# Retention followed by a multiplicative feed-forward layer: 2048-byte query rows, one marker copy per step, and a reordered start

## The chip, the cores and the metric

One core of one Trainium2 chip runs the whole program. The metric is the device time of one execution in microseconds; lower is better. The time before is 187.18 us, the median of three runs (186.01 to 188.56).

## What is computed

For 4 batches and 8 heads with 768 tokens of 64 numbers, a state of 64 x 64 numbers per head decays by a factor and takes in one key and one value per token; each query reads it. The heads of a token then stand side by side as a row of 512 numbers, which goes through four matrices.

```python
gamma = 1.0 - 2.0 ** (-5.0 - np.arange(H))          # H = 8, D = 64, S = 768
for t in range(S):
    state = gamma * state + outer(k[:, :, t], v[:, :, t])
    y[:, :, t] = 1/sqrt(D) * (q[:, :, t] @ state)
x = y.transpose(0, 2, 1, 3).reshape(B * S, H * D)   # 3072 x 512
out = ((x @ w1) * (x @ w2)) @ w3 @ w_out            # 512 -> 1024 -> 1024 -> 512
```

All inputs and the output are float32; the kernel computes its products in fp16 with float32 sums.

## The kernel before

The 3072 tokens are worked in twelve steps of 256 tokens, three for each batch. The order of all work is written out by hand, engine by engine, in the program text: every call of a helper issues its instructions at that place of its engine's queue.

**The start.** w3 and w_out are multiplied into one 1024 x 512 matrix, kept as eight tiles `W3O`. For this the rows of w3 are loaded (`load_rows`, L95), cast to fp16 (`cast_w3`, L228), turned by TensorE (`turn_w3`, L233), copied out of PSUM (`turned_w3`, L240), multiplied with the cast rows of w_out (`cast_wo`, `w3_mm`, L244) and copied out (`w3_out`, L257). Meanwhile GpSimd makes index tables and masks (`numbers`, `keeps`, `late_numbers`, `step_decays`), and ScalarE makes decay tables with the exponential (`tables` for the first two steps, `late_tables`, L215, for the later ones). `warm` (L610) issues products of zeros; eight of them stand at the very start.

**The loads.** SP's queue issues every transfer. `load` (L77) fetches 256 tokens of q, k or v as a tile of 128 partitions x 1024 float32 numbers from a ring of 18 such stage buffers. For the queries, and for all three inputs in steps 0 and 1 (`n < EO`), partition p holds the tokens 2p and 2p + 1 of each of the eight heads, in runs of 512 bytes (L84). For the keys and values of later steps partition i holds token i of each half of the 256, in runs of 256 bytes, with two transfers per tile (L89). Loads, turns and stores of several steps share the one queue in the order written: in the later steps it reads, per step, the turn of k for the next step, v of the step after that, the turn of q, k and q of a step further on, and the store of an earlier result.

**One step.** GpSimd casts q and k to fp16 (`cast`, L266) and scales and casts v (`cast_v`, L278). From step 4 on a DMA transposes the cast tiles into `qT` and `kT` (`dma_turn`, L297, L300); before that TensorE does it (`turn`, `turned`). `kv` (L364) makes the sums of outer products, `state` (L397) carries the state on, `scores` (L324) makes the products of keys and queries, `mask` (L347) cuts the future off. `inter` (L428) multiplies queries with the states; it has two halves, `part` 0 and 1, which write the two halves of the partitions of the same PSUM banks. Between them `fence` (L457) lets ScalarE copy one column of each of the two banks to a scratch tile (L463), and the second half waits for these marker copies. `av` (L465) adds the products of the masked scores with the values, and `x_out` (L486) scales the result into `XT`, the 512 x 256 input of the feed-forward layer. The products of 64 x 64 numbers run four at a time in the quarters of TensorE's array. `qchunk` (L320) cuts the queries of 64 tokens out of `qT`, as two runs of 32 numbers.

**The feed-forward layer.** `blk` with `evac` makes two of the eight row blocks of x @ w1 or x @ w2 (`two_blocks`, L511, L517): 64 products of 128 x 256 per step. VectorE multiplies the two into `HT`. `o_unit` (L567, L572) makes 128 rows of the output with eight products of 128 x 512, `o_copy` scales them, `o_store_all` (L599, L601) stores a step's 256 rows. From step 2 on TensorE's queue goes, per step: the first half of `inter` for step n, the first half of `kv` and the `scores` for n + 1, the second half of `inter`, `av`, the two `o_unit` of step n - 1, and then the `blk` of step n. Steps 0 and 1 use the same products spread out by rows of w1 and w2 as those land (`rows`, L541, L552).

Of the kernel before, what the change touches and what calls it, by code (L numbers as in the profile page):

```python
# [20 lines left out]
def kernel(  # L21
# [15 lines left out]
    EO = 2  # L37
# [39 lines left out]
    def load(nm, n, via=None):  # L77
        via = via or nc.sync
        b, c = divmod(n, PER)
        t = new_stage()  # L80
        src = source[nm][b, :, c * T : (c + 1) * T, :]
        if nm == "q" or n < EO:

            via.dma_start(  # L84
                t[:, :].rearrange("p (h x) -> p h x", x=2 * D), src.rearrange("h (p t) d -> p h (t d)", t=2)
            )
        else:
            for s in range(2):
                via.dma_start(  # L89
                    t[:, s * 512 : (s + 1) * 512].rearrange("p (h d) -> p h d", d=D),  # L90
                    src[:, s * 128 : (s + 1) * 128, :].rearrange("h i d -> i h d"),
                )
        tok_in[nm, n] = t
# [43 lines left out]
    def numbers():  # L137

        nc.gpsimd.iota(key_i[:, :, :], pattern=[[1, 2], [0, H]], base=1 - 128, channel_multiplier=2)
        nc.gpsimd.iota(  # L140
            col_i[:, :, :].rearrange("p g (t j) -> p g t j", t=2), pattern=[[128, 2], [1, 2], [2, 64]],
            base=1 - 128, channel_multiplier=0,
        )
        for h in range(H):
            p = h // 2
            c = place(p, h % 2) * 64
            nc.gpsimd.memset(LGH[:, h : h + 1], -math.log(gam[h]))
            nc.gpsimd.memset(LGP[c : c + 64, p : p + 1], math.log(gam[h]))

    def keeps():  # L150
        nc.gpsimd.memset(keep[:, :, :], 1.0)
        for g in range(2):
            rows = slice(g * 64, g * 64 + 64)
            for t in range(2):
                nc.gpsimd.affine_select(
                    out=keep[rows, t, :], in_=keep[rows, t, :], compare_op=GE, fill=0.0,
                    base=-t, pattern=[[1, 2], [2, 64]], channel_multiplier=-2,
                )

    def late_numbers():  # L160

        nc.gpsimd.iota(tok_i[:, :, :], pattern=[[128, 2], [0, H]], base=1 - 128, channel_multiplier=1)
        for g in range(2):
            nc.gpsimd.iota(
                pos_i[:, g, :, :].rearrange("p s (t i) -> p s t i", t=2), pattern=[[128, 2], [1, 2], [2, 32]],
                base=1 - 128 + 64 * g, channel_multiplier=0,
            )
        nc.gpsimd.memset(keep64[:, :], 1.0)
        for g in range(2):
            rows = slice(g * 64, g * 64 + 64)  # L170
            nc.gpsimd.affine_select(
                out=keep64[rows, :], in_=keep64[rows, :], compare_op=GE, fill=0.0,
                base=0, pattern=[[1, 2], [2, 32]], channel_multiplier=-1,
            )

    VS = const.tile([128, 2, H], FP, name="VS")
# [48 lines left out]
    def cast_wo(i, eng):  # L225
        copy(eng, WO[i][:, :, :].rearrange("p a n -> p (a n)"), wo_st[i][:, :])
# [39 lines left out]
    def cast(nm, n, eng):  # L266
        dst = {"q": q16, "k": k16}[nm]
        dst[n] = t = att.tile([128, 2, 512], HP, tag=nm + "16", name=nm + "16", bufs=3)
        src = tok_in.pop((nm, n))
        if nm == "q" or n < EO:  # L270
            copy(
                eng, t[:, :, :].rearrange("p t (h d) -> p h t d", d=D),
                src[:, :].rearrange("p (h t d) -> p h t d", t=2, d=D),
            )
        else:
            copy(eng, t[:, :, :].rearrange("p s c -> p (s c)"), src[:, :])
# [40 lines left out]
    def half(x):  # L317
        return slice(x * 64, x * 64 + 64)

    def qchunk(n, r, a, s, g):  # L320
        c = 2 * s + g
        return qT[n][half(r), :, a, c * 32 : (c + 1) * 32]

    def scores(n, tags, hp=None):  # L324
        if n < EO:
            ps = [bank(t, [128, 2, 2, 128]) for t in tags]
            for i in range(2):
                for t in range(2):
                    for r, g in QUARTERS:
                        a = hp * 2 + i  # L330
                        nc.tensor.matmul(
                            ps[r][half(g), i, t, :], lhsT=kT[n][half(r), t, a, half(g)],
                            rhs=qT[n][half(r), :, a, half(g)], start=True, stop=True,
                        )
        else:
            ps = [bank(t, [128, NP, 2, 64]) for t in tags]
            for a in range(NP):
                for s in range(2):
                    for r, g in QUARTERS:
                        nc.tensor.matmul(  # L340
                            ps[r][half(g), a, s, :], lhsT=kT[n][half(r), s, a, half(g)],
                            rhs=qchunk(n, r, a, s, g), start=True, stop=True,
                        )
        for r in range(2):
            am[n, hp, r] = ps[r]
# [82 lines left out]
    def inter(n, part, tags=None):  # L428
        assert state_n.get(n, 0) >= len(chunks(n)) - 1 and inter_n.get(n, 0) == part
        if part == 0:  # L430
            for g in range(2):
                X[n, g] = bank(tags[g], [128, NP, 128])
            X[n] = set()
        else:
            assert n in fenced
        inter_n[n] = part + 1
        begun = X[n]
        for i in range(NP // 2):
            for s in range(1 if n < EO else 2):
                for a in (2 * i, 2 * i + 1):  # L440
                    for g in range(2):
                        c = g if n < EO else (s, g)
                        if (n, c) not in TS:
                            continue
                        r = g ^ 1 ^ part
                        o = place(a, r)
                        if n < EO:
                            dst, rhs = X[n, g][half(o), a, :], qT[n][half(r), :, a, half(c)]
                        else:
                            dst, rhs = X[n, g][half(o), a, s * 64 : (s + 1) * 64], qchunk(n, r, a, s, g)  # L450
                        nc.tensor.matmul(  # L451
                            dst, lhsT=TS[n, c][half(r), a, :], rhs=rhs, start=((g, o) not in begun), stop=False,
                            skip_group_check=True,
                        )
                        begun.add((g, o))

    def fence(n):  # L457
        assert inter_n[n] == 1
        fenced.add(n)
        for g in range(2):  # L460
            if (g, g) in X[n]:
                t = att.tile([128, 1], FP, tag=f"fence{g}", name="fence")
                nc.scalar.copy(t[half(g), :], X[n, g][half(g), NP - 1, 64:65])  # L463

    def av(n):  # L465
        assert inter_n[n] == 2
# [19 lines left out]
    def x_out(n, g):  # L486
# [3 lines left out]
            XT[n] = att.tile([128, NP, T], HP, tag="xt", name="xt", bufs=3)  # L490
        x = X.pop((n, g))
        if n < EO:
            order = "p a (t i) -> p a t i"
            nc.vector.tensor_tensor(
                XT[n][:, :, g * 128 : (g + 1) * 128].rearrange("p a (i t) -> p a t i", t=2),
                x[:, :, :].rearrange(order, t=2), YS[:, g, :, :].rearrange(order, t=2), MULT,
            )
        else:
            nc.vector.tensor_tensor(  # L499
                XT[n][:, :, :].rearrange("p a (s x) -> p (a s) x", s=2)[:, :, g * 64 : (g + 1) * 64].rearrange(  # L500
                    "p k (i t) -> p k t i", t=2
                ),
                x[:, :, :].rearrange("p a (s t i) -> p (a s) t i", s=2, t=2),
                YN[:, g, :, :, :].rearrange("p a s (t i) -> p (a s) t i", t=2), MULT,
            )


# [165 lines left out]
    warm(8)  # L673
    identity()
    numbers()
    keeps()
    arguments()
    tables()
    cast_w3(4, "v")
    step_decays()  # L680
    turn_w3(4, "S0")
    late_numbers()
    cast_wo(0, "v")
    turned_w3(4, "s")
    late_arguments()
    w3_mm(4, 0, "S0", first=True)
    cast_w3(1, "v")
    late_tables()
    turn_w3(1, "S1")
    cast_w3(2, "g")  # L690
    turned_w3(1, "v")
    turn_w3(2, "X0")
    cast_wo(1, "g")
    w3_mm(1, 0, "S1", first=True)
    turned_w3(2, "s")
    w3_mm(1, 1)
    cast_w3(5, "v")
    w3_mm(4, 1)
    w3_mm(2, 1, "X0", first=True)
    w3_mm(2, 0)  # L700
    cast_wo(2, "g")
    turn_w3(5, "X1")
    turned_w3(5, "s")
    w3_mm(4, 2)
# [51 lines left out]
    w3_mm(6, 3, last=True)  # L756
    state(0, 1)
    w3_out(7, "s")
    inter(0, 0, ("S0", "X1"))
    fence(0)  # L760
    turn("q", 1, "S1")
# [114 lines left out]
    cast("q", 3, "g")  # L876
    turned("k", 3, "s")
    o_copy(1, 0)
    o_unit(1, 1, ("F2",))
    inter(2, 1)  # L880
    av(2)
    x_out(2, 0)
    x_out(2, 1)
    turn("q", 3, "S1")
    turned("q", 3, "v")
    cast_v(3, "g")
# [448 lines left out]
```

## Time and profile before

| what | value |
|---|---|
| median of three runs | 187.18 us (186.01 to 188.56) |
| the profiled execution, its own time | 186.13 us |
| its span, first to last instruction | 184.4 us |
| granted TensorE clock, mean | 0.991 |
| TensorE (PE) busy | 173.6 us, 94% |
| VectorE (DVE) busy | 97.7 us, 53% |
| ScalarE (ACT) busy | 67.5 us, 37% |
| GpSimd (POOL) busy | 66.6 us, 36% |
| DMA packets | 81,498, 40.23 MB, mean 218 GB/s |
| of these under 512 B, under 2 KB | 59,328 and 75,968 |
| q loads | 12 transfers of 512 KB, median 6.7 us from issue to landing |
| k and v loads | 40 of 256 KB (5.5 and 5.8 us), 4 of 512 KB (10.3 and 9.5 us) |
| turns of k and q by DMA | 8 and 8, 7.0 and 4.9 us |

The durations come from one profiled execution, whose span leaves out 1.7 us of its time. Engines work at the same time, so their busy times do not add up. A wait counts only where the engine that waits is one that others wait for.

### The profile page before, as it was taken

The page shows a single profiled execution, that of the slowest core. Times are in us where ns is not written, and L with a number is a line of the kernel's source. Part 1 is how long each engine was busy: PE and PEld are TensorE (multiplying, and loading weights), DVE is VectorE, ACT ScalarE, POOL GpSimd, SP SyncE. Part 2 cuts the span into 40 slices and gives each one's busy share as a digit, 9 for nine tenths or more (in the row PEclk, how much of TensorE's full clock was granted, in tenths as well). Part 3 has the DMA queues.
Part 4 walks back from the last instruction along what each step waited for, and adds up shares of the span by engine and source line. Part 5 has one row for each costly group of instructions (what it writes and reads, how often), then busy time and mean ns, then how long its engine had stood idle before and what let it go on. Part 6 is the DMA issues. An engine that isn't in the chain of part 4 may idle for free.

```text
span 184.4 us, 6033 instructions
## 1 busy us (share of the span) xinstructions
PE 173.6 (94%) x2616; PEld 124.1 (67%) x2616; DVE 97.7 (53%) x169; ACT 67.5 (37%) x126; POOL 66.6 (36%) x93
## 2 busy tenths in 40 slices
PE   7489999898999799999999999999999999999993
PEld 2255555577955587685885868858778587686872
DVE  2433689842745485738447465472673844644220
ACT  4634415664253421331333233323133142332332
POOL 7851248653546136726244235440354010000000
PEclk9969999999999999999999999999999999999999
DMA  5999999999999899999999999999999960150303
GB/s 203 368 420 360 320 302 326 400 349 236 181 256 247 183 167 231 193 183 245 167 236 231 169 285 200 229 244 183 271 222 178 243 228 4 36 195 4 116 0 114
DMA packets 81498, 40.23 MB, mean 218 GB/s; under 512 B 59328, under 2 KB 75968, under 8 KB 81472
## 3 DMA queue, kind: packets, MB, share of 16 engines
q1 hardware_dynamic: 81472, 39.85, 95.8%
q8 instruction: 20, 0.33, 0.8%
q14 instruction: 6, 0.05, 0.1%
HBM read 29.36 MB, written 6.29 MB: 193 GB/s over the span
## 4 chain that ended last, share of the span: by engine, by line
PE 73%; DMA 8%; SPq 7%; DVE 4%; POOL 3%; ACT 2%; issue 2%; DVEq 0%; ACTq 0%; POOLq 0%
PE psF L517 36%; PE psF L572 20%; DMA st<-in_k_dram 5%; SPq L97 5%; DMA st<-in_moe_w_dram 3%; PE psF L552 3%; PE psX L451 2%; PE psX L552 2%; SPq L84 2%; PE psX L572 2%; PE psS L340 2%; PE psX L478 1%; ACT w L61 1%; DVE t L64 1%; POOL v L64 1%
## 5 line engine op out<-in xcount | busy, mean ns | idle before, releaser
L517 PE MATMUL psF<-xt,w 128*128 128x256 f16 x640 | 72.0, 273 | 1.2 <-DVE xt L499 1.0
L517 PEld LDWEIGHTS <-w 128*128 128x128 f16 x640 | 62.5, 98 | 10.8 <-issue 1.6
L64 DVE TENSOR_TENSOR ht<-pa,psF 128x512 f16<-128x512 f32 x43 | 29.5, 686 | 45.4 <-PE psF L517 43.9
L61 ACT COPY pa<-psF 128x512 f32<-128x512 f32 x43 | 25.1, 585 | 45.4 <-PE psF L517 39.1
L572 PE MATMUL psF<-w3o,ht 128*128 128x512 f16 (+2 forms) x184 | 38.5, 361 | 0.1
L572 PEld LDWEIGHTS <-ht 128*128 128x128 f16 x208 | 19.1, 98 | 19.1 <-DVE xt L499 0.4
L64 POOL TENSOR_TENSOR v<-st,VN 128x1024 f16<-128x1024 f32 x10 | 19.0, 1901 | 24.5 <-DMA st<-in_v_dram 15.8
L590 ACT ACTIVATE osb<-psF 128x512 f32<-128x512 f32 (+2 forms) x22 | 12.3, 558 | 35.1 <-PE psF L572 35.1
L499 DVE TENSOR_TENSOR xt<-psX,YN 128x512 f16<-128x512 f32 x19 | 12.8, 720 | 7.2 <-PE psX L478 7.2
L64 POOL TENSOR_TENSOR t<-s,GS 128x256 f16<-128x256 f32 x8 | 5.8, 728 | 25.2 <-DVE s L64 25.1
L552 PEld LDWEIGHTS <-w 128*128 128x128 f16 x128 | 11.9, 98 | 4.3 <-POOL w L61 1.3
L61 POOL CAST k<-st 128x1024 f16<-128x1024 f32 x11 | 11.4, 1036 | 8.3 <-DMA st<-in_k_dram 8.3
L61 POOL CAST q<-st 128x1024 f16<-128x1024 f32 x11 | 11.4, 1039 | 7.4 <-DMA st<-in_q_dram 4.9
L357 DVE TENSOR_TENSOR am<-psS,keep 128x512 f16<-128x512 f32 x19 | 12.2, 679 | 1.3 <-PE psF L340 1.3
L252 PEld LDWEIGHTS <-w3t 128*128 128x128 f16 x64 | 5.7, 101 | 7.3 <-ACT w3t L61 1.6
L552 PE MATMUL psF<-xt,w 128*128 128x256 f16 x56 | 9.7, 273 | 0.0
L451 PEld LDWEIGHTS <-t 64*64 64x64 f16 x320 | 5.7, 106 | 4.6 <-issue 2.9
L451 PE MATMUL psX<-qT,t 64*64 64x64 f16 (+1 forms) x296 | 8.3, 199 | 0.4 <-DVE t L64 0.2
L237 PEld LDWEIGHTS <-w3h 128*128 128x128 f16 x64 | 4.6, 113 | 4.9 <-DVE w3h L61 3.3
L552 PE MATMUL psX<-xt,w 128*128 128x256 f16 x32 | 6.1, 274 | 1.2 <-POOL w L61 0.6
L61 DVE CAST w3h<-st 128x1024 f16<-128x1024 f32 x5 | 3.5, 701 | 5.8 <-DMA st<-in_moe_w_dram 5.8
L64 DVE TENSOR_TENSOR t<-psK,t 128x256 f16<-128x256 f32 x15 | 6.2, 415 | 0.4
(121 smaller groups left out, 183.1 us busy)
## 6 DMA issues: line engine op xcount, KB each, us to landing
st<-in_moe_w_dram SPq DMA_DIRECT2D x16, 512.0 KB, 8.6
st<-in_q_dram SPq DMA_DIRECT2D x12, 512.0 KB, 6.7
st<-in_k_dram SPq DMA_DIRECT2D x20, 256.0 KB, 5.5
st<-in_v_dram SPq DMA_DIRECT2D x20, 256.0 KB, 5.8
out_dram<-osb SPq DMA_DIRECT2D x9, 512.0 KB, 5.5
st<-in_moe_w_out_dram SPq DMA_DIRECT2D x4, 512.0 KB, 7.8
st<-in_k_dram SPq DMA_DIRECT2D x2, 512.0 KB, 10.3
st<-in_v_dram SPq DMA_DIRECT2D x2, 512.0 KB, 9.5
```

Source lines behind the costliest of these rows:

```text
L61: {"v": nc.vector.tensor_copy, "g": nc.gpsimd.tensor_copy, "s": nc.scalar.copy}[eng](dst, src)
L64: (nc.vector if eng == "v" else nc.gpsimd).tensor_tensor(dst, a, b, op)
L97: nc.sync.dma_start(t[:, :], src[i * 128 : (i + 1) * 128, :])
L237: nc.tensor.transpose(ps[:, g * 128 : (g + 1) * 128], src[:, c0 : c0 + 255 : 2], ident16[:, :])
L252: nc.tensor.matmul(acc[f][:, :], lhsT=w3t[f][:, g * 128 : (g + 1) * 128], rhs=WO[i][:, r, :], start=(first and r == 0), stop=(last and r = ...
L357: nc.vector.tensor_tensor(t[:, :, :, :].rearrange("p a s i -> p (a s) i"), ps[:, :, :, :].rearrange("p a s i -> p (a s) i"), keep64[:, :]. ...
L451: nc.tensor.matmul(dst, lhsT=TS[n, c][half(r), a, :], rhs=rhs, start=((g, o) not in begun), stop=False, skip_group_check=True,)
L499: nc.vector.tensor_tensor(XT[n][:, :, :].rearrange("p a (s x) -> p (a s) x", s=2)[:, :, g * 64 : (g + 1) * 64].rearrange("p k (i t) -> p k ...
L517: nc.tensor.matmul(ps[:, i, :], lhsT=W[d][:, f * 128 : (f + 1) * 128], rhs=XT[n][:, d, :], start=(i == 0 and d == 0), stop=(i == 1 and d = ...
L552: nc.tensor.matmul(rows_ps[w, n, uh][j // 2][:, j % 2, :], lhsT=W[d][:, f * 128 : (f + 1) * 128], rhs=XT[n][:, d, :], start=(first and j % ...
L572: nc.tensor.matmul(ps[:, :], lhsT=HT[n][:, f, tb * 128 : (tb + 1) * 128], rhs=W3O[f][:, c0:c1], start=(f == 0), stop=(f == 7),)
L590: nc.scalar.activation(o_tile(n, tb)[:, c0:c1], o_ps.pop((n, tb, c0, c1))[:, :], AF.Copy, scale=final_scale)
```

## The change

- **Query loads.** A query tile is loaded by two transfers instead of one, one for the even heads and one for the odd heads. A partition now holds eight tokens of one head, 2048 bytes in one run: 4 heads x 32 groups of tokens make the 128 partitions. The cast puts even and odd heads of the same token side by side, so that the turned tile holds the tokens in eight groups (token modulo 8), and for each group the four head pairs with 32 tokens.
- **What follows from that order.** `queries` takes the place of `qchunk`: eight runs of 16 numbers in steps 0 and 1, eight runs of 8 numbers later. The column tables, the masks and the reading order of `x_out` follow the new order of tokens; `x_out` writes every eighth number in a row instead of every second.
- **Marker copies.** `fence` copies one column of one bank instead of two, and the second half of `inter` takes the two banks in the opposite order.
- **The start.** Some casts and copies change engines; `keeps`, `step_decays` and `late_numbers` stand later in GpSimd's queue, `late_arguments` and `late_tables` behind `w3_out(7)`; ten more products of zeros stand in TensorE's queue between the first turns of w3.
- **One moved block.** `o_unit(1, 1)` stands behind `x_out(2)` instead of before the second half of `inter(2)`.

```diff
         src = source[nm][b, :, c * T : (c + 1) * T, :]
-        if nm == "q" or n < EO:
+        if nm == "q":
+            for r in range(2):
+                via.dma_start(
+                    t[:, r * 512 : (r + 1) * 512], src[r::2, :, :].rearrange("a (u j) d -> a u (j d)", j=8)
+                )
+        elif n < EO:
             via.dma_start(
                 t[:, :].rearrange("p (h x) -> p h x", x=2 * D), src.rearrange("h (p t) d -> p h (t d)", t=2)
             )
...
-        if nm == "q" or n < EO:
+        if nm == "q":
+            copy(
+                eng, t[:, :, :].rearrange("p t x -> p (t x)").rearrange("p (j r d) -> p r j d", r=2, d=D),
+                src[:, :].rearrange("p (r j d) -> p r j d", r=2, d=D),
+            )
+        elif n < EO:
...
-    def qchunk(n, r, a, s, g):
-        c = 2 * s + g
-        return qT[n][half(r), :, a, c * 32 : (c + 1) * 32]
+    def queries(n, r, a, c):
+        x = qT[n][half(r), :, :, :].rearrange("p t a i -> p (t a i)").rearrange("p (j a u) -> p j a u", j=8, a=NP)
+        w = 16 if n < EO else 8
+        return x[:, :, a, c * w : (c + 1) * w]
...
-                    for g in range(2):
+                    for g in ((0, 1), (1, 0))[part]:
...
-        for g in range(2):
-            if (g, g) in X[n]:
-                t = att.tile([128, 1], FP, tag=f"fence{g}", name="fence")
-                nc.scalar.copy(t[half(g), :], X[n, g][half(g), NP - 1, 64:65])
+        assert (1, 1) in X[n]
+        t = att.tile([128, 1], FP, tag="fence", name="fence")
+        nc.scalar.copy(t[half(1), :], X[n, 1][half(1), NP - 1, 64:65])
...
                 XT[n][:, :, :].rearrange("p a (s x) -> p (a s) x", s=2)[:, :, g * 64 : (g + 1) * 64].rearrange(
-                    "p k (i t) -> p k t i", t=2
+                    "p k (u j) -> p k j u", j=8
                 ),
...
     identity()
     numbers()
-    keeps()
     arguments()
     tables()
     cast_w3(4, "v")
-    step_decays()
+    keeps()
     turn_w3(4, "S0")
-    late_numbers()
-    cast_wo(0, "v")
-    turned_w3(4, "s")
-    late_arguments()
+    warm(3, "F2")
+    turned_w3(4, "v")
+    cast_wo(0, "s")
     w3_mm(4, 0, "S0", first=True)
+    warm(1, "F2")
     cast_w3(1, "v")
-    late_tables()
     turn_w3(1, "S1")
-    cast_w3(2, "g")
-    turned_w3(1, "v")
+    warm(3, "F2")
+    turned_w3(1, "s")
+    cast_w3(2, "v")
     turn_w3(2, "X0")
+    warm(1, "F2")
     cast_wo(1, "g")
     w3_mm(1, 0, "S1", first=True)
-    turned_w3(2, "s")
+    warm(2, "F2")
+    turned_w3(2, "v")
...
     cast_wo(2, "g")
+    late_numbers()
+    step_decays()
...
     w3_out(7, "s")
+    late_arguments()
+    late_tables()
     inter(0, 0, ("S0", "X1"))
     fence(0)
...
-    o_unit(1, 1, ("F2",))
     inter(2, 1)
     av(2)
     x_out(2, 0)
     x_out(2, 1)
+    o_unit(1, 1, ("F2",))
```

More of the change, by code (lines that the diff above doesn't have):

```diff
@@ L140, in numbers @@
         nc.gpsimd.iota(
-            col_i[:, :, :].rearrange("p g (t j) -> p g t j", t=2), pattern=[[128, 2], [1, 2], [2, 64]],
+            col_i[:, :, :].rearrange("p g (j u) -> p g j u", j=8), pattern=[[128, 2], [1, 8], [8, 16]],
             base=1 - 128, channel_multiplier=0,
@@ L156, in keeps @@
                     out=keep[rows, t, :], in_=keep[rows, t, :], compare_op=GE, fill=0.0,
-                    base=-t, pattern=[[1, 2], [2, 64]], channel_multiplier=-2,
+                    base=-t, pattern=[[1, 8], [8, 16]], channel_multiplier=-2,
                 )
@@ L164, in late_numbers @@
             nc.gpsimd.iota(
-                pos_i[:, g, :, :].rearrange("p s (t i) -> p s t i", t=2), pattern=[[128, 2], [1, 2], [2, 32]],
+                pos_i[:, g, :, :].rearrange("p s (j u) -> p s j u", j=8), pattern=[[128, 2], [1, 8], [8, 8]],
                 base=1 - 128 + 64 * g, channel_multiplier=0,
@@ L172, in late_numbers @@
                 out=keep64[rows, :], in_=keep64[rows, :], compare_op=GE, fill=0.0,
-                base=0, pattern=[[1, 2], [2, 32]], channel_multiplier=-1,
+                base=0, pattern=[[1, 8], [8, 8]], channel_multiplier=-1,
             )
@@ L332, in scores @@
                             ps[r][half(g), i, t, :], lhsT=kT[n][half(r), t, a, half(g)],
-                            rhs=qT[n][half(r), :, a, half(g)], start=True, stop=True,
+                            rhs=queries(n, r, a, g), start=True, stop=True,
                         )
@@ L341, in scores @@
                             ps[r][half(g), a, s, :], lhsT=kT[n][half(r), s, a, half(g)],
-                            rhs=qchunk(n, r, a, s, g), start=True, stop=True,
+                            rhs=queries(n, r, a, 2 * s + g), start=True, stop=True,
                         )
@@ L447, in inter @@
                         if n < EO:
-                            dst, rhs = X[n, g][half(o), a, :], qT[n][half(r), :, a, half(c)]
+                            dst, rhs = X[n, g][half(o), a, :], queries(n, r, a, c)
                         else:
-                            dst, rhs = X[n, g][half(o), a, s * 64 : (s + 1) * 64], qchunk(n, r, a, s, g)
+                            dst, rhs = X[n, g][half(o), a, s * 64 : (s + 1) * 64], queries(n, r, a, 2 * s + g)
                         nc.tensor.matmul(
@@ L492, in x_out @@
         if n < EO:
-            order = "p a (t i) -> p a t i"
+            order = "p a (j u) -> p a j u"
             nc.vector.tensor_tensor(
-                XT[n][:, :, g * 128 : (g + 1) * 128].rearrange("p a (i t) -> p a t i", t=2),
-                x[:, :, :].rearrange(order, t=2), YS[:, g, :, :].rearrange(order, t=2), MULT,
+                XT[n][:, :, g * 128 : (g + 1) * 128].rearrange("p a (u j) -> p a j u", j=8),
+                x[:, :, :].rearrange(order, j=8), YS[:, g, :, :].rearrange(order, j=8), MULT,
             )
@@ L500, in x_out @@
                 XT[n][:, :, :].rearrange("p a (s x) -> p (a s) x", s=2)[:, :, g * 64 : (g + 1) * 64].rearrange(
-                    "p k (i t) -> p k t i", t=2
+                    "p k (u j) -> p k j u", j=8
                 ),
-                x[:, :, :].rearrange("p a (s t i) -> p (a s) t i", s=2, t=2),
-                YN[:, g, :, :, :].rearrange("p a s (t i) -> p (a s) t i", t=2), MULT,
+                x[:, :, :].rearrange("p a (s j u) -> p (a s) j u", s=2, j=8),
+                YN[:, g, :, :, :].rearrange("p a s (j u) -> p (a s) j u", j=8), MULT,
             )
```

## The prediction

> **What bounds the kernel now.** I read the busy times in stretches first, then the chain of waits, then the queue of DMA issues (SP), then the DMA packets. The stretches (columns: from:to and length in us, busy us of PE, PEld, DVE, ACT, POOL with their instruction counts, granted clock, DMA share, GB/s):
>
> ```profile
> 0.00:15.50 15.50, 11.00 (x57) 5.51 (x58) 4.56 (x10) 7.88 (x14) 10.37 (x46) 0.89 0.89 330
> 15.50:34.00 18.50, 17.47 (x249) 9.54 (x247) 13.96 (x23) 7.40 (x12) 8.76 (x7) 1.00 1.08 334
> 62.00:141.00 79.00, 77.80 (x1330) 59.31 (x1330) 45.83 (x81) 24.81 (x51) 31.72 (x27) 1.00 1.26 212
> 141.00:184.40 43.40, 40.28 (x592) 30.47 (x589) 18.76 (x31) 13.65 (x29) 1.91 (x2) 1.00 0.33 111
> ```
>
> From 62 us on PE is 98% busy, and the chain of waits holds almost nothing but PE: one step of 256 tokens takes 11.85 us (o_unit of two steps starts at 84.22 and 96.08). Before 34 us the chain runs through DMA, and the DMA engines are never idle after 3 us. But the DMA side is close behind PE up to 141 us as well. The SP queue in order of time (start, us, operation) has hardly a gap:
>
> ```profile
> 118.43 3.19 SPq L300 DMA_TRANSPOSE kT<-k  x1
> 121.67 2.36 SPq L89 DMA_DIRECT2D st<-in_v_dram  x2
> 124.14 3.19 SPq L300 DMA_TRANSPOSE qT<-q  x1
> 127.38 1.21 SPq L89 DMA_DIRECT2D st<-in_k_dram  x2
> 128.63 0.85 SPq L84 DMA_DIRECT2D st<-in_q_dram  x1
> 129.58 1.08 SPq L601 DMA_DIRECT2D out_dram<-osb  x1
> 130.76 2.74 SPq L300 DMA_TRANSPOSE kT<-k  x1
> ```
>
> This is one step of the queue, 12.3 us against PE's 11.85. The turned queries of step 10 are issued at 136.07 and land about 4.9 us later (the median of the qT tile's transfers), at 141.0; PE starts scores(10) at 142.87. So the queries arrive only **1.9 us** before PE needs them, and all twelve query loads stand ahead of that transpose in the same queue. Some room is left in the queue's waits for POOL and ACT from 62 to 141 us (us, times, longest): 15.7 us in all, in six lines of which these are the largest.
>
> ```profile
> SPq L300 <- POOL q L61: 5.9, 4, 2.1
> SPq L300 <- POOL t L64: 3.3, 1, 3.3
> SPq L300 <- POOL v L64: 2.4, 1, 2.4
> ```
>
> The packets' prices come from stretches with one size of row: 512-byte rows at 26 to 28 us, 256-byte rows at 46 to 48, 2048-byte rows (stores) at 160 to 166 (of these the queue's packets, MB and share of 16 engines).
>
> ```profile
> DMA packets 1145, 0.58 MB, mean 289 GB/s; under 512 B 17, under 2 KB 1145, under 8 KB 1145
> ...
> DMA packets 1693, 0.44 MB, mean 221 GB/s; under 512 B 1692, under 2 KB 1692, under 8 KB 1692
> ...
> q1 hardware_dynamic: 560, 1.05, 46.2%
> ```
>
> A sixteenth of 289 GB/s is 18.1 bytes a ns, so a 512-byte row costs an engine **28.3 ns**. At 221 GB/s a 256-byte row costs 18.5 ns. The stores: 0.462 x 16 x 6 us over 512 rows is 86 ns; weight rows of 4096 bytes ran at 421 GB/s (10 to 13 us), so half of one is 78 ns. A **2048-byte row costs 78 to 86 ns**; I take 82.
>
> **The query loads.** Before, a load is one transfer of 128 x 8 rows of 512 bytes: 1024/16 = 64 rows for each of 16 engines, 64 x 28.3 = 1.8 us. After, it is two transfers whose source has dimensions 4 x 32 x 2048 bytes (four heads, 32 groups of eight tokens) and whose destination has 128 partitions. How such a transfer is shared over the engines no row shows, because every copy of before has 128 as the outermost dimension on both sides. That those used all 16 engines fits the packet counts: 59,328 packets are under 512 B; the k and v loads from step 2 on (40 x 1024) and 16 transposes of 1024 leave 1,984 = 16 x (108 + 16), sixteen end markers for each of 108 copies and 16 transposes, if a transpose has two rounds. The bounds: shared over 16 engines, a load is 256/16 = 16 rows each, 16 x 82 = 1.3 us, 0.5 us **less** than now. Shared along the outermost dimension, four heads can feed four engines only: 256/4 = 64 rows each, 64 x 82 = **5.3 us on four engines**, 3.5 us more (3.2 to 3.7), and nothing on the other twelve. I take four engines: all 108 copies had an outermost size that 16 divides, this one has not, and a split along it needs no new cut of the pattern.
>
> By the Trainium skill (DMA: Bandwidth & Descriptors, section "Why a DMA increments its semaphore by 16 and not by 1") a hardware-issued DMA runs on the largest number of engines up to 16 that divides the slowest dimension of both patterns, and on the lowest-numbered ones. The rule gives 4 here, the same four for every load; the sixteen markers per copy of before agree with it.
>
> A transfer is complete when its slowest engine is, and every engine works its queue in order, so the four loaded engines set the time of all that follows. Per step they would carry k 128 x 18.5 = 2.4, v 2.4, two transposes 2.4, a store 16 x 86 ns = 1.4 and q 5.3 us: 13.9 us against PE's 11.85; today it is 10.4. That is how **DMA becomes the bound**. Over twelve loads: 12 x 3.5 = 42 us (38 to 44). Off that: 1.9 us of lead of the queries, and the engines' free time before 141 us. That is 62 to 141 us less packet work, 79 - 67 = 12 us, and about 1 us earlier. The 67 us are 42,300 rows at 18.5, 7,168 at 28.3 and 1,024 at 82 ns, over 16. Not all of it can be used, as the queue stays held while a transpose runs (2.58 us median for kT): I take 8 of 13 us. Where the delay goes: the weights behind q0 and q1 land 7 us late, so the first W product (34.0 us) moves to about 41; after that each further load adds up to 3.5 us, and scores(n) waits for qT(n). Behind that wait stand masks, av, x_out and all of W1 and W2 on PE. After scores(10) PE's own 41.5 us to the end follow unchanged.
>
> **The other edits.** SP issues twelve more transfers, 12 x 0.44 us, while it stands blocked by full queues: nothing. The query cast keeps 1024 elements and runs of 64 (POOL q, 1039 ns), and the eight-wide tables and masks keep their sizes: nothing. Ten zero products of 128 x 512 (0.22 us at full clock, 0.43 at half) fill up to 4 us of the 5.5 us that PE idles before 34 us (4.5 and 1.0 in the first two stretches). The clock is granted at 0.50 around 10 to 12 us, which costs PE about 1.7 us, but the chain there is DMA, so I count 0; uncovered it would be 1.7. One marker of ACT instead of two: 0.15 us a step, hidden by kv and scores between the two halves of inter. o_unit(1, 1) behind x_out(2) fills the 1.6 us that PE waits for xt at 61.3 to 62.9; under late queries it gains nothing. late_tables (about 1.9 us of ACT) moves from 8 us to before the marker of step 0, which gates inter(0, 1): 0 to 2 us late at 29 us, hidden by the late k1. x_out writes with a step of 16 bytes: today's step of 4 bytes costs 721 ns against 679 for the contiguous mask, so 0 to 0.7 us each if it doubled, hidden behind o_unit (3.56 us).
>
> **Sum.** 184.4 + 42 - 1.9 - 8 = 216.5 us of span; the profiled execution took 186.13 us, 1.7 more than its span, so **218 us**. That execution lies 0.6% below the median of 187.18.
>
> **Rivals.** First, the same transfers spread over all 16 engines. It decides if the split isn't bound to the outermost dimension. Then each load is 0.5 us shorter, the two ahead of the weights give 1.0 us, o_unit up to 1.6, late_tables takes 0 to 2: span 182 to 185, time 184 to 186, which is **no slower** than before. For it: the destination keeps 128 partitions. Against it: the source's outermost 4. Second, sixteen engines, but products that read queries in runs of eight fp16 are slow: inter and scores take about 0.8 us a step; doubled over ten steps that is +8 us, 192 us. No row shows runs shorter than 32 elements. The Trainium skill (SBUF — State Buffer, section "Door 1: The DMA port swizzle") says that accesses within a 16-byte line run at full bandwidth, and eight fp16 are one line; by it this rival falls away. Third, four engines but hidden, because 18 buffers load up to three steps ahead: it decides only if 38 us or more were free, and the rows show 13 + 1.9. With all of that used and 38 us of extra work: 207.9 + 1.7 = 210 us, so still slower; this is the low end of my forecast. The high end: 44 us, 3 us recovered, and 3 us for a clock that falls at the waits and for transposes that wait longer: 229 us.
>
> **How the numbers follow.** Four engines: 0.86 (209 to 230). Sixteen engines: 0.09, of which 0.03 faster by over 2% (what a measurement of this kernel can tell from no change). Slow short runs: 0.05, slower. So faster 0.03, within 2% 0.06, slower 0.91. The range is 206 to 230: four engines, with the prices and the recovered time at their ends and a little more below.
>
> **What would show it.** Four engines: the main queue's packets fall from 81,472 to 72,160 (-12 x 1024 + 24 x 128 data rows, -192 + 96 end markers); on sixteen they would be 72,448. The query loads' median from issue to landing rises above 8 us (6.7 now), loads and transposes run past 170 us, PE waits 2 to 4 us before the scores of each step from 5 on, and the rows of W1 and W2 start near 41 us. Query loads landing sooner than now, with the first W product at or before 34 us, would prove me wrong; so would L340 and L451 products clearly above 194 ns.

## The result, and the profile after

The changed kernel takes 230.06 us (median of four runs, 229.46 to 232.85) against 186.86 us, the kernel before with a fourth run: a ratio of 1.233 (95% interval 1.219 to 1.246). It is slower, as forecast, and by more: 230.06 us lies just above the range's end of 230. The profiled execution took 229.46 us, with a span of 227.8 us against 184.4.

Packets first: the page's count, and the main queue's packets, MB and share of 16 engines.

```profile
DMA packets 72185, 40.22 MB, mean 177 GB/s; under 512 B 59232, under 2 KB 63584, under 8 KB 72160
...
q1 hardware_dynamic: 72160, 39.85, 86.9%
```

72,160 is the count that the prediction gave for four engines, to the packet; sixteen would have left 72,448. The bytes are the same. A stretch in which only a query load runs, 30.5 to 32 us, shows the rate (an answer on DMA for that stretch alone):

```profile
DMA packets 77, 0.15 MB, mean 100 GB/s; under 512 B 4, under 2 KB 4, under 8 KB 77
...
q1 hardware_dynamic: 77, 0.15, 26.3%
```

A share of 26% is what four engines out of sixteen would give, and the packets of this stretch confirm it: at each moment four of them are under way, for a fifth of the time five, and each takes 84 to 93 ns. At 100 GB/s each of the four moves 25 bytes a ns, so a row of 2048 bytes takes 82 ns, and the 64 rows of a query tile take 5.2 us on each of them, while twelve engines stand still. The rule of the Trainium skill (DMA: Bandwidth & Descriptors, section "Why a DMA increments its semaphore by 16 and not by 1") agrees with this trace: the source's outermost size was 4, and the count holds four end markers for each of the 24 transfers (72,064 + 24 x 4 = 72,160).

The stretches of time (columns as in the prediction) show who waits:

```profile
15.50:34.00 18.50, 14.02 (x151) 7.35 (x148) 10.06 (x18) 3.37 (x6) 4.58 (x10) 0.91 0.75 211
...
62.00:141.00 79.00, 67.63 (x1098) 47.39 (x1095) 51.59 (x64) 20.78 (x37) 26.21 (x22) 0.96 1.10 164
141.00:184.40 43.40, 36.22 (x602) 26.65 (x601) 29.37 (x36) 10.48 (x20) 13.18 (x11) 0.97 1.20 180
184.40:227.80 43.40, 36.29 (x449) 27.01 (x447) 24.29 (x28) 12.46 (x24) 0.73 (x1) 0.99 0.23 84
```

PE was 98% busy from 62 to 141 us; now it is 86%, with 164 GB/s moved instead of 212. VectorE is busier (51.6 us against 45.8) although it ran fewer instructions (64 against 81). The granted TensorE clock, 0.99 on the mean before, is 0.95. One step of the SP queue:

```profile
137.38 4.73 SPq L310 DMA_TRANSPOSE kT<-k  x1
142.17 3.26 SPq L94 DMA_DIRECT2D st<-in_v_dram  x2
145.53 1.95 SPq L310 DMA_TRANSPOSE qT<-q  x1
147.53 1.20 SPq L94 DMA_DIRECT2D st<-in_k_dram  x2
148.77 2.88 SPq L84 DMA_DIRECT2D st<-in_q_dram  x2
151.76 0.45 SPq L611 DMA_DIRECT2D out_dram<-osb  x1
152.31 4.47 SPq L310 DMA_TRANSPOSE kT<-k  x1
```

From the first turn of k at 82.25 us to the seventh at 165.83, six steps take 13.93 us each; the prediction's sum for a loaded engine was 13.9. The waits (engine, operation, line, who was waited for: us, times, longest) name a second cause beside the loads:

```profile
POOL v L64 <- DMA st<-in_v_dram: 32.3, 10, 8.4
...
POOL q L61 <- DMA st<-in_q_dram: 26.9, 6, 5.9
...
PE psF L527 <- DVE xt L509: 11.8, 7, 3.0
...
PE psS L351 <- DMA qT<-q: 8.0, 5, 2.7
```

PE waits for the turned queries, and longer for `XT`. The group of x_out says why, before and after: 2536 ns each, against 720.

```profile
L499 DVE TENSOR_TENSOR xt<-psX,YN 128x512 f16<-128x512 f32 x19 | 12.8, 720 | 7.2 <-PE psX L478 7.2
...
L509 DVE TENSOR_TENSOR xt<-psX,YN 128x512 f16<-128x512 f32 x19 | 44.8, 2536 | 17.0 <-PE psX L488 17.0
```

### The profile page after: what moved, and what is told of

Read it like the earlier page. It is cut to its first block, busy times and chain, and to the rows that moved or that the text cites. A ratio compares the mean times of both kernels' runs of the same rounds, so it can differ in the third digit from the quotient of the medians.

```text
span 227.8 us, 6038 instructions
## 1 busy us (share of the span) xinstructions
PE 187.0 (82%) x2626; PEld 128.2 (56%) x2626; DVE 137.8 (60%) x170; ACT 65.7 (29%) x115; POOL 65.3 (29%) x92
## 2 busy tenths in 40 slices
DMA packets 72185, 40.22 MB, mean 177 GB/s; under 512 B 59232, under 2 KB 63584, under 8 KB 72160
## 3 DMA queue, kind: packets, MB, share of 16 engines
q1 hardware_dynamic: 72160, 39.85, 86.9%
## 4 chain that ended last, share of the span: by engine, by line
DMA 34%; PE 28%; SPq 16%; DVE 8%; issue 7%; POOL 6%; ACT 0%; POOLq 0%; DVEq 0%
DMA st<-in_q_dram 21%; PE psF L527 11%; SPq L102 5%; DMA st<-in_k_dram 5%; PE psF L582 5%; SPq L310 4%; SPq L94 4%; DVE xt L509 4%; SPq L84 3%; DMA qT<-q 3%; DMA st<-in_moe_w_dram 3%; PE psF L562 3%; DMA st<-in_v_dram 2%; DVE xt L504 2%; POOL k L61 2%
## 5 line engine op out<-in xcount | busy, mean ns | idle before, releaser
L527 PE MATMUL psF<-xt,w 128*128 128x256 f16 x640 | 71.9, 273 | 13.2 <-DVE xt L509 11.8
L527 PEld LDWEIGHTS <-w 128*128 128x128 f16 x640 | 61.9, 98 | 24.4 <-DVE xt L509 12.5
L509 DVE TENSOR_TENSOR xt<-psX,YN 128x512 f16<-128x512 f32 x19 | 44.8, 2536 | 17.0 <-PE psX L488 17.0
L582 PE MATMUL psF<-w3o,ht 128*128 128x512 f16 (+2 forms) x184 | 43.2, 392 | 0.0
L582 PEld LDWEIGHTS <-ht 128*128 128x128 f16 x208 | 20.3, 103 | 22.5 <-issue 6.6
L600 ACT ACTIVATE osb<-psF 128x512 f32<-128x512 f32 (+2 forms) x22 | 12.3, 559 | 51.6 <-PE psF L582 51.6
L562 PEld LDWEIGHTS <-w 128*128 128x128 f16 x128 | 13.5, 108 | 8.1 <-issue 4.0
L257 PEld LDWEIGHTS <-w3t 128*128 128x128 f16 x64 | 6.3, 106 | 9.0 <-issue 3.7
L562 PE MATMUL psF<-xt,w 128*128 128x256 f16 x56 | 11.1, 303 | 0.0
L351 PE MATMUL psS<-qT,kT 64*64 64x64 f16 x304 | 4.5, 194 | 8.0 <-DMA qT<-q 8.0
L351 PEld LDWEIGHTS <-kT 64*64 64x64 f16 x320 | 4.1, 108 | 10.4 <-issue 8.1
L61 DVE CAST w3h<-st 128x1024 f16<-128x1024 f32 x6 | 4.4, 734 | 6.8 <-DMA st<-in_moe_w_dram 6.8
L562 PE MATMUL psS<-xt,w 128*128 128x256 f16 x24 | 5.3, 343 | 3.4 <-DVE xt L504 3.4
```

Source lines behind the costliest of these rows:

```text
L61: {"v": nc.vector.tensor_copy, "g": nc.gpsimd.tensor_copy, "s": nc.scalar.copy}[eng](dst, src)
L509: nc.vector.tensor_tensor(XT[n][:, :, :].rearrange("p a (s x) -> p (a s) x", s=2)[:, :, g * 64 : (g + 1) * 64].rearrange("p k (u j) -> p k ...
L527: nc.tensor.matmul(ps[:, i, :], lhsT=W[d][:, f * 128 : (f + 1) * 128], rhs=XT[n][:, d, :], start=(i == 0 and d == 0), stop=(i == 1 and d = ...
L562: nc.tensor.matmul(rows_ps[w, n, uh][j // 2][:, j % 2, :], lhsT=W[d][:, f * 128 : (f + 1) * 128], rhs=XT[n][:, d, :], start=(first and j % ...
L582: nc.tensor.matmul(ps[:, :], lhsT=HT[n][:, f, tb * 128 : (tb + 1) * 128], rhs=W3O[f][:, c0:c1], start=(f == 0), stop=(f == 7),)
L600: nc.scalar.activation(o_tile(n, tb)[:, c0:c1], o_ps.pop((n, tb, c0, c1))[:, :], AF.Copy, scale=final_scale)
```

## The experiments

### The two causes, alone and together (e1, e2, e3)

e1 loads a query tile by four transfers of 32 partitions, so that the outermost size is 32 on both sides:

```diff
-            for r in range(2):
+            for a in range(NP):
                 via.dma_start(
-                    t[:, r * 512 : (r + 1) * 512], src[r::2, :, :].rearrange("a (u j) d -> a u (j d)", j=8)
+                    t[a * 32 : (a + 1) * 32, :].rearrange("p (r x) -> p r x", r=2),
+                    src[2 * a : 2 * a + 2, :, :].rearrange("r (u j) d -> u r (j d)", j=8),
                 )
```

> The changed kernel with one edit: a query tile is loaded by four transfers of 32 partitions x 2 rows of 2048 bytes (one per head pair) instead of two transfers with a source of 4 x 32 rows. Rows, bytes and everything behind the load stay the same. Theory (two causes, the engine split first): 32 is divided by 16, so all 16 DMA engines share each load, the main queue has 72256 - 96 + ... = 72,832 packets (72,064 data rows and end markers before the query loads, plus 48 x 16 markers), a load costs an engine about 1.3 us, and DMA is no longer what PE waits for. What is left is the slow x_out (2.5 us instead of 0.72 us, two per step): about 1 to 2 us a step behind the cover of o_unit (3.56 us). Span 195 to 206 us. Rival (the slow x_out sets the steps by itself, and the loads are late only because the steps are): hardly any gain, 220 us or more. Rival (it is the 2048-byte rows themselves, not the split): 220 us or more as well, with query loads landing as late as now.

e2 lets x_out write contiguous numbers and step through PSUM instead. The iotas of the decay tables lose their step, so the tables lie in token order, and the branch of steps 0 and 1 changes in the same way; shown is the branch of the later steps:

```diff
...
-                    "p k (u j) -> p k j u", j=8
+                    "p k (u j) -> p k u j", j=8
                 ),
-                x[:, :, :].rearrange("p a (s j u) -> p (a s) j u", s=2, j=8),
-                YN[:, g, :, :, :].rearrange("p a s (j u) -> p (a s) j u", j=8), MULT,
+                x[:, :, :].rearrange("p a (s j u) -> p (a s) u j", s=2, j=8),
+                YN[:, g, :, :, :].rearrange("p a s (u j) -> p (a s) u j", j=8), MULT,
...
```

> The changed kernel with one edit: x_out writes XT in a run of contiguous numbers and reads PSUM out of order instead (step of 8 numbers), with the decay tables in token order. The loads on four engines stay. Theory (engine split first, x_out second): the steps stay at about 13.9 us, scores(10) still starts near 180 us, and only the tail behind it shortens from 47.4 us to about 41.5 us if the read order costs nothing: span 221 to 224 us. Rival (x_out sets the steps): 185 to 200 us. If reading PSUM with a step is as slow as writing SBUF with one, nothing changes: 227 to 229 us.

e3 has both edits.

> Both edits together: four transfers of 32 partitions per query tile, and x_out writing contiguous numbers. Theory (these two are the whole loss): back to the kernel before or a little under it, since 2048-byte rows save 0.5 us per load and o_unit(1, 1) covers x_out(2): span 181 to 185 us, time 183 to 187 us. Rival (a third cause, such as products reading queries in runs of eight, or the reordered start): 190 us or more, and L351 or L462 above 194 ns or the first W product behind 35 us would show which.

| span of the profiled execution, us (ratio of the times to before, interval) | x_out writes every eighth number | x_out writes contiguous numbers |
|---|---|---|
| loads on four engines | 227.8, the change (1.233) | 222.4, e2 (1.193, 1.184 to 1.202) |
| loads on sixteen engines | 214.1, e1 (1.158, 1.149 to 1.167) | 188.1, e3 (1.012, 1.004 to 1.019) |

Each cause alone costs a great deal: the loads 222.4 - 188.1 = 34.3 us, the writes 214.1 - 188.1 = 26.0 us. Together they cost 39.7 us and not 60.3, because the slower of the two paces a step and hides most of the other: a step takes 13.25 us with slow writes alone (e1), 14.1 us with loads on four engines alone (e2, by the turns of k from 81.13 to 165.85 us), and 13.9 us with both. In e1 PE waits for x_out in nine of the ten steps from step 2 on (the chain: start, us, what):

```profile
128.45 2.00 issue
130.44 2.64 DVE xt L510
133.09 0.05 issue
133.13 7.16 PE psF L528 x64
```

The next block of 64 products starts at 146.38, so a step takes 13.25 us: 11.85, and 1.4 of waiting, since two x_out of about 2.5 us do not fit behind two o_unit (3.56 us). "issue" there is most of the first x_out, which the chain does not name. The packets of e1 are 72,832, the count for sixteen engines. I expected 195 to 206 us and got 214.1. Against e3 the W products of step 2 start 7.4 us later (74.7 against 67.3 us), and 18.6 us more are lost behind them: 12.0 in eight waits of PE for x_out, 2.9 in one for another VectorE instruction (the state of step 3), and the rest is not broken down.

e3, expected at 181 to 185 us, takes 188.1. Its first W product starts at 39.1 us, and a start behind 35 was named as the sign of a third cause; e6 to e11 look for it.

e2 is the kernel of which the prediction's sum speaks, with x_out covered. Its chain near the end:

```profile
174.27 5.31 DMA qT<-q
...
179.63 0.45 PE psS L351 x32
...
180.72 5.21 PE psF L582 x16
```

scores(10) start at 179.63 us, about as in the change (180.42), and the end follows 42.8 us later, not 47.4. So x_out's share, with the loads as they are, is mostly the 4.6 us behind the last late transpose, out of 5.4 us between the two spans. The two o_unit shown (16 products) take 5.21 us instead of 3.56, because the clock granted to TensorE is 0.50 from 182 to 184 us, in e2 as in the change. It follows a wait of PE for the queries (1.9 us in the change, 2.6 in e2); that the wait brings it about, no run shows.

### What of the access pattern is slow (e4)

e4 is the kernel before with another pattern for x_out in each step; the tokens of steps 2 to 8 land in another order.

```diff
...
+            write, read, table = {
+                2: (1, 1, 1), 3: (4, 1, 1), 4: (8, 1, 1), 5: (16, 1, 1), 6: (1, 2, 1), 7: (1, 8, 1), 8: (1, 1, 8),
+            }.get(n, (2, 1, 1))
...
```

> The kernel before, where x_out uses another access pattern in each of steps 2 to 8: write contiguous (step 2), write with a step of 4, 8 and 16 numbers (steps 3, 4, 5), read PSUM with a step of 2 and 8 numbers (steps 6, 7), read the table with a step of 8 numbers (step 8); steps 9 to 11 write with a step of 2 as before. The tokens of steps 2 to 8 stand in another order in the result. Theory (the write step is what costs, as the bytes between two numbers grow): 680 ns contiguous, 721 ns at 2, some value between at 4, 2.5 us at 8 and no less at 16; reads at 0.7 us. Rival (it is the short inner run of eight, whatever is stepped): the reads with a step of 8 are as slow as the writes with a step of 8.

The two x_out of steps 3 to 8, in that order (min/median/max ns, then the first and last start):

```profile
L509 DVE TENSOR_TENSOR xt<-psX,YN x2: 1307/1328/1348, 72.9 to 74.0; 128x512 f16<-128x512 f32 x2
...
L509 DVE TENSOR_TENSOR xt<-psX,YN x2: 2435/2532/2630, 85.7 to 87.7; 128x512 f16<-128x512 f32 x2
...
L509 DVE TENSOR_TENSOR xt<-psX,YN x2: 2333/2424/2514, 99.0 to 101.0; 128x512 f16<-128x512 f32 x2
...
L509 DVE TENSOR_TENSOR xt<-psX,YN x2: 680/685/690, 112.2 to 112.8; 128x512 f16<-128x512 f32 x2
...
L509 DVE TENSOR_TENSOR xt<-psX,YN x2: 680/686/692, 124.0 to 124.6; 128x512 f16<-128x512 f32 x2
...
L509 DVE TENSOR_TENSOR xt<-psX,YN x2: 1064/1068/1071, 137.3 to 138.3; 128x512 f16<-128x512 f32 x2
```

Writing fp16 with a step of 4 numbers (8 bytes) takes 1328 ns, of 8 (16 bytes) 2532, of 16 (32 bytes) 2424; a step of 2 took 721 before, and contiguous writes in e2 681. Stepping through PSUM costs nothing (685), stepping through the float32 table in SBUF something (1068). So the write's step is the cause and not the short inner run, and the price rises steeply between 4 and 16 bytes. The prediction had extended the price of 4 bytes.

### Only the outermost size decides (e5)

e5 keeps two transfers of 128 rows, contiguous writes in x_out, and turns two dimensions of the query source round:

```diff
-                    t[:, r * 512 : (r + 1) * 512], src[r::2, :, :].rearrange("a (u j) d -> a u (j d)", j=8)
+                    t[:, r * 512 : (r + 1) * 512], src[r::2, :, :].rearrange("a (u j) d -> u a (j d)", j=8)
...
-        x = qT[n][half(r), :, :, :].rearrange("p t a i -> p (t a i)").rearrange("p (j a u) -> p j a u", j=8, a=NP)
+        x = qT[n][half(r), :, :, :].rearrange("p t a i -> p (t a i)").rearrange("p (j u a) -> p j u a", j=8, a=NP)
         w = 16 if n < EO else 8
-        return x[:, :, a, c * w : (c + 1) * w]
+        return x[:, :, c * w : (c + 1) * w, a]
```

> The changed kernel with x_out writing contiguous numbers, and with the query source taken in the order 32 x 4 instead of 4 x 32: still two transfers of 128 rows of 2048 bytes per tile, with the partition now holding (group of tokens, head pair) instead of (head pair, group of tokens). The queries of a product then stand four numbers apart in the turned tile. Theory (only the outermost size decides how many engines share a transfer): 32 is divided by 16, so all 16 engines work; the query loads land in under 7 us, the main queue has 72,064 + 24 x 16 = 72,448 packets, and the span is 182 to 188 us, less than the 188.1 us of the four-transfer version by the start, whose transfers reach 32 partitions each. Rival (2048-byte rows are slow in any such transfer): 215 us or more. Rival (queries that stand 8 bytes apart slow TensorE down): L352-like products above 194 ns and 190 us or more.

The same rows and bytes now take 4.7 us from issue to landing, the queue has the 72,448 packets expected, and 15.5 to 34 us move 369 GB/s (211 in the change, 334 before). e2 differs from e5 only in this order and in the matching reads of the queries; against it the span falls from 222.4 to 189.3 us. The ratio to the kernel before is 1.014 (1.009 to 1.018). What it loses instead shows in the score products, of e5 and then of e2:

```profile
L351 PE MATMUL psS<-qT,kT x304: 212/230/235, 58.5 to 159.9; 64*64 64x64 f16 x152
...
L351 PE MATMUL psS<-qT,kT x304: 186/193/258, 63.9 to 193.4; 64*64 64x64 f16 x152
```

Queries 8 bytes apart make a product of 64 columns 230 ns instead of 193, and a step about 12.1 us (o_unit at 75.06, 87.14, 99.24). Runs of eight queries, 16 bytes, cost nothing: 193 against 194 ns before. I expected 182 to 188 us, and 190 or more if slow queries were to count; the span was 189.3, so the slow queries do count.

### The start, the marker and the moved block (e6 to e9)

e6 is the kernel before with the new start alone, e9 the same with the tables further back (e9 against e6):

```diff
...
     w3_out(7, "s")
-    late_arguments()
-    late_tables()
...
     rows_out("a", 0, 0, 0, "s")
+    late_arguments()
+    late_tables()
...
```

> The kernel before with the new start alone: ten more zero products, the casts and copies on other engines, keeps, step_decays and late_numbers later, late_arguments and late_tables behind w3_out(7). Theory: the half clock of 9 to 12.7 us goes, the chain there is DMA so this gains nothing, and late_tables puts 1.9 us of ACT in front of the marker of step 0, which PE waits for: span 185 to 187 us, 0.5 to 2.5 us longer. Rival (the warm clock is worth something): 182 to 184 us.

> The kernel before with the new start, but late_arguments and late_tables put further back, behind the copy of the last W1 block of step 0 (ACT idles 2.9 us there). Theory (the two tables in front of the marker are what the new start costs): the marker of step 0 runs at about 28.9 us instead of 30.8, and the span is 184 to 185 us, the 1.8 us of the new start gone. Rival (the swapped engines or zero products cost it): still 186 us.

e6: 186.2 us of span, ratio 1.009 (1.006 to 1.012). Its chain shows the tables ahead of the marker:

```profile
28.87 0.20 ACT VN L216
29.07 1.69 ACT YN L218 x4
30.79 0.16 ACT fence L463
30.99 0.24 PE psX L451 x2
```

e9: 184.9 us, 1.002 (0.998 to 1.005). The new start costs 1.8 us of span, and 1.3 us of that go away when these 1.9 us of ScalarE stand further back. The clock is full from the beginning in e6 (0.50 at 10 to 12 us before), and that wins nothing that e6 or e9 shows; the chain there is DMA.

e7 changes the marker alone, e8 moves o_unit(1, 1) alone (diffs as in the change).

> The kernel before with one marker copy per step alone. Theory: 0.15 us of ACT hidden behind kv and scores: 184.4 us within 0.3. Rival (PE waits for the second marker in each step): 182 to 183.5 us.

> The kernel before with o_unit(1, 1) behind x_out(2) alone. Theory: PE's wait for xt at 61.3 to 62.9 us is filled: span 182.8 to 183.6 us. Rival (the DMA and DVE work behind it are late anyway): 184.4 us.

e7: 184.3 us of span, 0.998 (0.994 to 1.002). e8: 1.000 (0.996 to 1.003). Neither is a difference that can be measured. That o_unit fills PE's wait of 1.6 us without shortening the run fits the rival, work behind it that is late anyway; e12 below shows which.

### What is left over (e10, e11, e12)

e10 is e3 with the start of before, e11 is e3 with the tables further back as in e9.

> The changed kernel with four transfers per query tile, contiguous writes in x_out and the start of before: what is left of the change is 2048-byte query rows, runs of eight queries, one marker and o_unit(1, 1). Theory (the rest of the 188.1 us is the start, about 1.8 us): 185.5 to 187 us of span. Rival (transfers into 32 partitions make the first loads late): the start stays behind, 187 to 189 us, and DMA moves less than 300 GB/s from 15.5 to 34 us as it did with the new start (282).

> The changed kernel with four transfers per query tile, contiguous writes in x_out, and the tables behind the last W1 block of step 0. Theory: as the version with the old start or a little less, 185 to 187 us of span. Rival: 188 us, if the tables were covered by the late query loads there anyway.

e10: 186.8 us of span, 1.010 (1.006 to 1.015). e11: 188.8 us, 1.012 (1.005 to 1.018). The span of e10 lies where I expected it, but its ratio can't be told from that of e3 (1.012) or e11, so in this version the runs show no price of the start; e11 came out at its rival's 188 us. In e10 the second query load moves at 130 to 300 GB/s in the slices of 20 to 21.5 us (transfers into 32 partitions), and the first W product starts at 35.0 us instead of 34.0. By step 2 that is made up: its W products start at 62.7 us, 62.9 before. The 2.4 us are lost behind that, where PE waits four times, 3.2 us in all, for turned queries; in the kernel before it never does. Why they come late there stays open.

e12 is the kernel before with the marker, the moved o_unit and contiguous writes in x_out.

> The kernel before with the three edits that cost nothing so far: one marker per step, o_unit(1, 1) behind x_out(2), and x_out writing contiguous numbers with the decay tables in token order (0.68 us instead of 0.72 each). Theory (all three lie beside other work): 184.4 us of span within 0.7, a ratio between 0.994 and 1.002. Rival (x_out stands in front of PE in the last step, where only 1.83 us cover it, and the wait at 61 us is filled): 182 to 183.5 us, a ratio of 0.985 to 0.993.

e12: 184.9 us of span, 0.996 (0.993 to 1.000), at the edge of nothing. Its trace shows where the 1.6 us of the moved o_unit go. The W products of step 2 start at 61.4 us instead of 62.9, but from then on PE waits twice for turned queries, 0.7 us at 70 and 2.3 us at 118 to 120, for which it did not wait before. With DMA as close behind PE as the prediction found it, what PE wins it waits for later. No version was clearly faster than the kernel before.

## Why the prediction was right and wrong

- **Four engines: right.** The packet count, four packets at a time and 82 ns a row agree with the sum, and e5 shows that the outermost size decides. (The prediction's 108 copies are 92 copies and 16 transposes; with two rounds per transpose its sum of 16 x 124 markers stays.)
- **DMA becomes the bound: right.** 13.9 us a step were worked out and 13.93 measured. That they meet so closely is luck, as the steps of the change wait for x_out too; with x_out fast (e2) it is 14.1. The first W product came at 43.3 us, not 41; 1.1 us of that is the slow x_out, as it came at 42.2 in e2. One sign failed: PE was to wait 2 to 4 us before the scores of each step from 5 on, and waited five times, 8.0 us in all. Part of the delay stood in its waits for x_out instead; in e2 it waited seven times, 21.2 us.
- **The recovered free time: mis-sized.** 42 - 8 = 34 us of delay were forecast for the turned queries of step 10; they were issued at 174.06 instead of 136.07, 38 us later. So, if the loads cost the 42 us, about 4 us were recovered and not 8, which is near the 3 us of the high end: from 82 to 180 us the SP queue still waited 20 us for POOL, while POOL's casts waited for loads.
- **The bound on x_out failed.** "0 to 0.7 us each if it doubled, hidden behind o_unit" became 1.8 us each, and two of them (5.1 us) do not fit behind 3.56 us. This is the step that put the time above the range: with contiguous writes (e2) the median is 223.2 us, inside it. The bound came from one row, a step of 4 bytes, and was extended to 16 bytes as if nothing could jump between them.
- **"PE's own 41.5 us to the end follow unchanged" failed with it.** It took 47.4 us: 4.6 more from x_out, and 1.3 more that e2 has as well, where the two o_unit behind the late scores ran at a granted clock of 0.50 (5.21 us instead of 3.56). The sum had nothing for the clock, only the high end had. With 4 us less recovered, 216.5 us become 226.4 of the 227.8 measured; turned queries that took 6.3 us to land instead of 4.9 are the rest. These terms are read from this one trace, and those of the loads are not measured apart.
- **The rivals.** Sixteen engines: no. Loads hidden by the buffers: no. Slow runs of eight queries: no, 193 ns. The Trainium skill (SBUF — State Buffer, section "Door 1: The DMA port swizzle") has accesses within a 16-byte line at full rate. TensorE's reads of eight fp16 in a row agree (193 ns). Its reads with a step of 8 bytes, two in each line, do not (230 ns in e5), and VectorE's writes do not: two fp16 in each line already took 1328 ns, so here the measurement decides.
- **The small edits.** The marker is hidden, as forecast. late_tables cost 1.3 us of the "0 to 2 us" where no late loads cover it (e6 against e9). The 1.6 us of o_unit(1, 1) are won at step 2 and lost again to waits for turned queries (e12).

## What to carry to other kernels

Before a load is cut into longer rows, look at the outermost dimension of both its patterns: an outermost size of four took twelve of sixteen engines away, and cost far more (34 us) than the longer rows could give (an estimated 0.5 us a load). A new order of data must be priced at every reader and writer, and a step that no row of the trace has needs a measurement or a wide bound: here the step was free when read out of PSUM and made the instruction 3.5 times as long when written to SBUF. Two stalls in one loop hide each other, so undo them one at a time and together.

## What the runs showed that I had not expected

- VectorE's write of 512 fp16 per partition: 681 ns contiguous, 721 at 4 bytes of step, 1328 at 8, 2532 at 16, 2424 at 32; PSUM reads with a step of 8 or 32 bytes 685 and 686.
- TensorE's product of 64 moving columns: 193 ns in runs of 16 bytes, 230 ns with a step of 8 bytes.
- Loads into 32 partitions at a time, on all sixteen engines, left the stretch from 15.5 to 34 us at 282 GB/s in e3, where 128 partitions moved 369 in e5.
